# Float32 products of a retention and SiLU kernel as three one-pass products of 12-bit halves, in two parts

## The chip, the cores and the metric

The kernel runs on one core of one Trainium2 chip. The metric is the device time of one execution in microseconds (us); lower is better. The engines of a core run side by side, each through its own list of instructions in order: PE (TensorE, matmuls, with its weight loads shown apart as PEld), DVE (VectorE), ACT (ScalarE), POOL (GpSimd) and SP (SyncE, which here only issues DMAs). They wait for one another through semaphores.

## The reference

Attention by a recurrent state with decay, then a two-layer network with SiLU; B, H, S, D = 4, 8, 768, 64, d_model = 512, d_ff = 2048.

```python
for t in range(S):
    state = gamma * state + einsum('bhd,bhe->bhde', k[:, :, t], v[:, :, t])
    y[:, :, t] = scale * einsum('bhd,bhde->bhe', q[:, :, t], state)
x = y.transpose(0, 2, 1, 3).reshape(B * S, H * D)      # 3072 x 512
h = x @ w_in                                            # 512 x 2048
g = h * (1.0 / (1.0 + np.exp(-h)))
out = g @ w_out                                         # 2048 x 512
```

q, k, v are float32. The two weights arrive as float64 (a product of float32 noise with a float64 factor), so the kernel gets them as 64-bit words and rounds them to float32 itself.

## The kernel before

The 768 positions are cut into six chunks c of 128; a chunk of all four batches b is 512 tokens. A unit is one (c, b); its attention has four stages: `stage_t` (scaling of q on DVE and of v on POOL, transposes of k and q on PE, copies on ACT), `stage_a` (the scores, masked on DVE), `stage_y` (the output, transposed, copied into `xt[c]` by ACT) and `stage_s` (the update of the state on DVE; left out for the last chunk).

The network works in slices f of 128 of the 2048 hidden columns, 16 per chunk. `product_in(c, f)` makes h for a slice: four float32 matmuls of 128x128 weights with 128x512 tokens into one PSUM bank, then a sigmoid on ACT and one DVE multiplication give g. `product_out` multiplies a slice of g with the same slice of w_out, four matmuls into four banks `op[b]` that gather over all 16 slices; `store` copies them out at the end of a chunk. So per slice PE does eight float32 matmuls of 512 columns. In the trace each of them stands as two MATMUL records with two weight loads.

`product_out` runs one slice behind `product_in`, and one attention stage of chunk c + 1 stands after each slice of chunk c, so that a unit takes four slices. All weights stay on chip as float32 in `w_sb`, 16 tiles. `convert_w(f)` makes slice f of both weights out of the 64-bit words, eight DVE instructions over 1024 elements each; slices 0 to 3 are made during the attention of chunk 0 and the others during the 16 slices of chunk 0, four slices ahead of their use. Three staging tiles hold the words on their way in.

The order on each engine is set by the framework's scheduler from the order in which the code is written; on an engine nothing overtakes. Nearly all DMAs are issued by SP, in its order, and the stores of the result by ACT.

## Time and profile before

| | |
|---|---|
| time, 3 runs | 818.97 us median (816.91 to 819.06) |
| span of the profiled execution | 818.2 us |
| PE busy | 789.4 us, 96% of the span |
| DVE / ACT / POOL busy | 269.9 / 107.2 / 30.3 us |
| matmuls of the network, L263 and L273 | 768 + 768 records |
| DMA | 42.42 MB, mean 52 GB/s |

The span goes from the first to the last instruction, and the median of the runs is 0.8 us above it. A busy PE is not PE at its peak, since records of matmuls overlap; so the pace of a stream of matmuls is read from the chain of waits, where a group has the time that it advances the chain, and not from the mean of one record.

### The profile page before, as it was taken

How to read it: one execution, taken by the hardware profiler on the slowest of the kernel's cores; microseconds unless marked ns; L12 is line 12 of the kernel's file. 1: busy time of each engine (PE TensorE's matmuls, PEld its weight loads, DVE VectorE, ACT ScalarE, POOL GpSimd, SP SyncE). 2: the span in 40 equal slices, each digit the busy share in tenths (PEclk: the TensorE clock that was granted, in tenths of full speed). 3: DMA queues.
4: the chain of work that ended last, by engine and by line, in shares of the span. 5: the costliest groups of instructions: out<-in, count | busy, mean ns of one | idle time of the engine just before them, and what ended most of it. 6: DMA issues, size and time to landing. Idle time of an engine off the chain costs nothing.

```text
span 818.2 us, 7374 instructions
## 1 busy us (share of the span) xinstructions
PE 789.4 (96%) x3136; PEld 392.2 (48%) x3136; DVE 269.9 (33%) x398; ACT 107.2 (13%) x184; POOL 30.3 (4%) x36
## 2 busy tenths in 40 slices
PE   4789999999999999999999999999999999999997
PEld 3654445444544454545444544544454445444443
DVE  5889999922112112211122122111311111111111
ACT  1120111101111111011111110110111111100001
POOL 2100000000000000000000000000000000000000
PEclk9999999999999999999999999999999999999999
DMA  9868544102101103011011111000100000100001
GB/s 227 223 160 215 152 132 153 50 8 84 29 11 39 26 14 91 14 25 40 0 39 49 41 39 26 1 14 1 64 1 1 0 1 1 51 0 1 0 0 52
DMA packets 89121, 42.42 MB, mean 52 GB/s; under 512 B 75776, under 2 KB 83968, under 8 KB 89088
## 3 DMA queue, kind: packets, MB, share of 16 engines
q1 hardware_dynamic: 85632, 35.66, 17.5%
q10 hardware_dynamic: 3456, 6.29, 2.1%
q8 instruction: 24, 0.39, 0.2%
q14 instruction: 9, 0.07, 0.0%
HBM read 35.65 MB, written 6.29 MB: 51 GB/s over the span
## 4 chain that ended last, share of the span: by engine, by line
PE 84%; DVE 12%; issue 1%; DMA 1%; ACT 1%; SPq 0%; DVEq 0%; ACTq 0%
PE h L263 37%; PE op L273 35%; PE sc L205 3%; PE y L229 3%; PE y L225 2%; DVE w L137 2%; DVE ct L129 2%; DVE cp L133 2%; DVE ct L135 2%; PE s L243 1%; PE qtp L194 1%; PE ktp L194 1%; DVE ca L124 1%; DVE ca L122 1%; DVE am L211 1%
## 5 line engine op out<-in xcount | busy, mean ns | idle before, releaser
L263 PE MATMUL h<-xt,w 128*128 128x512 f32 x768 | 351.9, 601 | 0.0
L273 PE MATMUL op<-w,g 128*128 128x512 f32 x768 | 345.1, 593 | 0.0
L273 PEld LDWEIGHTS op<-w,g 128*128 128x128 f32 x768 | 146.2, 190 | 183.3 <-issue 182.2
L263 PEld LDWEIGHTS h<-xt,w 128*128 128x128 f32 x768 | 140.2, 191 | 154.0 <-issue 150.3
L268 DVE TENSOR_TENSOR g<-h,sg 128x512 f32<-128x512 f32 x96 | 66.3, 691 | 395.5 <-ACT sg L266 395.4
L266 ACT ACTIVATE sg<-h 128x512 f32<-128x512 f32 x96 | 57.3, 597 | 498.0 <-PE h L263 490.9
L229 PE MATMUL y<-am,vs 128*64 128x128 f32 x384 | 42.1, 299 | 10.3 <-DVE am L211 10.3
L188 POOL TENSOR_TENSOR vs<-vf,gk 128x512 f32<-128x512 f32 x24 | 27.5, 1144 | 599.4 <-PE s L243 530.2
L211 DVE TENSOR_TENSOR am<-sc,mask 128x512 f32<-128x512 f32 x48 | 31.3, 686 | 52.7 <-PE sc L205 52.7
L205 PEld LDWEIGHTS sc<-qt,kt 64*128 64x128 f32 x384 | 26.6, 210 | 19.6 <-issue 15.2
L229 PEld LDWEIGHTS y<-am,vs 128*64 128x64 f32 x384 | 28.7, 151 | 12.9 <-issue 9.2
L205 PE MATMUL sc<-qt,kt 64*128 64x128 f32 x384 | 31.6, 310 | 2.8 <-ACT qt L196 2.8
L225 PE MATMUL y<-qt,state 128*64 128x128 f32 x320 | 32.6, 279 | 0.0
L232 ACT COPY xt<-y 128x512 f32<-128x512 f32 x24 | 14.1, 586 | 124.5 <-PE y L229 124.5
L185 DVE TENSOR_TENSOR qs<-qf,gq 128x512 f32<-128x512 f32 x24 | 16.6, 690 | 38.1 <-PE qtp L194 37.5
L225 PEld LDWEIGHTS y<-qt,state 128*64 128x64 f32 x320 | 19.9, 136 | 15.2 <-issue 13.6
L250 DVE TENSOR_TENSOR state<-state,s 64x256 f32<-64x256 f32 x32 | 13.4, 417 | 36.1 <-PE s L243 35.6
L196 ACT COPY kt<-ktp 128x512 f32<-128x512 f32 x24 | 14.0, 585 | 66.7 <-PE ktp L194 66.7
L194 PE MATMUL ktp<-ident,kf 128*128 128x128 f32 x96 | 16.4, 299 | 5.4 <-DMA kf<-in_k_dram 5.4
L194 PE MATMUL qtp<-ident,qs 128*128 128x128 f32 x96 | 16.5, 300 | 5.1 <-DVE state L250 2.9
L194 PEld LDWEIGHTS ktp<-ident,kf 128*128 128x128 f32 x96 | 12.9, 154 | 16.3 <-issue 15.9
L243 PEld LDWEIGHTS s<-vs,kf 128*64 128x64 f32 x320 | 14.8, 154 | 12.1 <-issue 12.1
(32 smaller groups left out, 210.2 us busy)
## 6 DMA issues: line engine op xcount, KB each, us to landing
wf<-in_moe_w_in_dram SPq DMA_DIRECT2D x16, 512.0 KB, 4.3
wf<-in_moe_w_out_dram SPq DMA_DIRECT2D x16, 512.0 KB, 5.2
qf<-in_q_dram SPq DMA_DIRECT2D x24, 256.0 KB, 4.1
kf<-in_k_dram SPq DMA_DIRECT2D x24, 256.0 KB, 3.1
vf<-in_v_dram SPq DMA_DIRECT2D x24, 256.0 KB, 4.2
out_dram<-o ACTq DMA_DIRECT2D x24, 256.0 KB, 2.0
```

Source lines behind the costliest of these rows:

```text
L185: nc.vector.tensor_tensor(out=qs, in0=qf, in1=gq.unsqueeze(2).to_broadcast([128, H, D]), op=ALU.mult)
L188: nc.gpsimd.tensor_tensor(out=vs, in0=vf, in1=gk.unsqueeze(2).to_broadcast([128, H, D]), op=ALU.mult)
L194: nc.tensor.transpose(tp[:, a, :], src[:, 2 * a : 2 * a + 2, :], ident)
L205: nc.tensor.matmul(ap[j][:, a, :], lhsT=u["kt"][ts(j, D), a, :], rhs=u["qt"][ts(j, D), a, :], start=True, stop=True, skip_group_check=True)
L211: nc.vector.tensor_tensor(out=am, in0=ap[j], in1=mask.unsqueeze(1).to_broadcast([128, HP, C]), op=ALU.mult)
L225: nc.tensor.matmul(yp[ts(j, D), a, :], lhsT=state[b][:, a, ts(j, D)], rhs=u["qt"][:, a, :], start=True, stop=False, skip_group_check=True)
L229: nc.tensor.matmul(yp[ts(j, D), a, :], lhsT=u["vs"][:, 2 * a + j, :], rhs=u["am"][j][:, a, :], start=(c == 0), stop=True, skip_group_check ...
L243: nc.tensor.matmul(sp[ts(j, D), a, :], lhsT=u["kf"][:, h, :], rhs=u["vs"][:, h, :], start=True, stop=True, skip_group_check=True)
L263: nc.tensor.matmul(hp, lhsT=w_sb[f][:, 0, ts(kk, 128)], rhs=xt[c][:, kk, :], start=(kk == 0), stop=(kk == KIN - 1))
L266: nc.scalar.activation(out=sg, in_=hp, func=AF.Sigmoid)
L268: nc.vector.tensor_tensor(out=g, in0=hp, in1=sg, op=ALU.mult)
L273: nc.tensor.matmul(op[b], lhsT=g[:, ts(b, C)], rhs=w_sb[f][:, 1, :], start=(f == 0), stop=(f == NF - 1))
```

## The change

Every float32 value that goes into a product of the network is split into a high half of 12 bits and a low half, both held as `float32r`, a form of float32 that the tensor engine takes in one pass. With high h, low l and a scaled combination m, x @ w is built from three matmuls (h with h, l with the scaled low of w, and m with m), gathered in two PSUM banks, `ha` (`oa`) and `hb` (`ob`); the result is `ONE_E * ha - hb`. The attention keeps its float32 matmuls.

The kernel is cut in two. The first part makes g for all six chunks and writes it to DRAM (96 tiles of 128x512 float32); the second reads it back and makes the output. The 16 weight tiles `w{f}` (three 128x512 each) hold w_in's halves in the first part and w_out's in the second; w_out is rounded to float32 in the first part and also goes through DRAM.

```diff
+    def split_w(pool, f, w32, name):
+        w = wpool.tile([128, 3, 512], FP32R, tag=f"w{f}", name=f"{name}{f}")
+        lo = pool.tile([128, 512], FP32, tag="wl", name=f"{name}l_{f}")
+        nc.scalar.activation(out=w[:, 0, :], in_=w32, func=AF.Copy, scale=HALF)
+        high = w[:, 0, :].bitcast(FP32)
+        nc.vector.tensor_tensor(out=lo, in0=w32, in1=high, op=ALU.subtract)
+        nc.scalar.activation(out=w[:, 1, :], in_=lo, func=AF.Copy, scale=1.0 / EPS)
+        nc.vector.scalar_tensor_tensor(out=w[:, 2, :], in0=high, scalar=EPS, in1=lo,
+                                       op0=ALU.mult, op1=ALU.subtract)
...
-    ld = ctx.enter_context(tc.tile_pool(name="ld", bufs=4))
-    work = ctx.enter_context(tc.tile_pool(name="work", bufs=2))
-    stage = ctx.enter_context(tc.tile_pool(name="stage", bufs=3))
+        ld = first.enter_context(tc.tile_pool(name="ld", bufs=2))
+        one = first.enter_context(tc.tile_pool(name="one", bufs=1))
+        work = first.enter_context(tc.tile_pool(name="work", bufs=2))
+        stage = first.enter_context(tc.tile_pool(name="stage", bufs=2))
...
-    ps_a = ctx.enter_context(tc.tile_pool(name="ps_a", bufs=2, space=PS))
+        ps_a = first.enter_context(tc.tile_pool(name="ps_a", bufs=4, space=PS))
...
+        def take_w(i):
+            w32 = convert_w(i)
+            if i < NF:
+                w_sb[i] = split_w(conv, i, w32, "wi")
+            else:
+                nc.sync.dma_start(out=wo_dram[i - NF], in_=w32)
...
-        nc.scalar.copy(out=xt[c][:, :, ts(b, C)], in_=yp)
+            nc.scalar.activation(out=xh, in_=yp, func=AF.Copy, scale=HALF)
+            nc.vector.tensor_tensor(out=xl, in0=yp, in1=xh.bitcast(FP32), op=ALU.subtract)
+            nc.vector.scalar_tensor_tensor(out=xm, in0=xl.bitcast(FP32), scalar=-1.0 / EPS,
+                                           in1=xh.bitcast(FP32), op0=ALU.mult, op1=ALU.add)
...
-            nc.tensor.matmul(hp, lhsT=w_sb[f][:, 0, ts(kk, 128)], rhs=xt[c][:, kk, :],
-                             start=(kk == 0), stop=(kk == KIN - 1))
-        nc.scalar.activation(out=sg, in_=hp, func=AF.Sigmoid)
-        nc.vector.tensor_tensor(out=g, in0=hp, in1=sg, op=ALU.mult)
+                nc.tensor.matmul(ha, lhsT=w[0], rhs=x[0], start=first_, stop=False)
+                nc.tensor.matmul(ha, lhsT=w[1], rhs=x[1], start=False, stop=last)
+                nc.tensor.matmul(hb, lhsT=w[2], rhs=x[2], start=first_, stop=last)
+            nc.scalar.activation(out=hs, in_=ha, func=AF.Copy, scale=ONE_E)
+            nc.vector.tensor_tensor(out=hs, in0=hs, in1=hb, op=ALU.subtract)
+            nc.scalar.activation(out=g, in_=hs, func=AF.Sigmoid)
+            nc.gpsimd.tensor_tensor(out=g, in0=hs, in1=g, op=ALU.mult)
+            pending.append((c, f, g))
+        def put_g(keep):
+            while len(pending) > keep:
+                c, f, g = pending.pop(0)
+                nc.sync.dma_start(out=g_dram[c, f], in_=g)
...
-            if before is not None:
-                product_out(*before)
-                if f == 0:
-                    store(c - 1, before[0])
-            if c == 0:
-                convert_w(f + 4)
+                if c == 0 or f % 4 == 1:
+                    take_w(taken)
+                    taken += 1
+                put_g(1)
...
+        def split(n):
+            get(n + G_AHEAD)
+            if c == 0:
+                wo[f] = split_w(wl, f, got.pop((n, "w")), "wo")
+            nc.scalar.activation(out=t[:, 0, :], in_=g, func=AF.Copy, scale=HALF)
+            nc.vector.tensor_tensor(out=t[:, 1, :], in0=g, in1=high, op=ALU.subtract)
+            nc.vector.scalar_tensor_tensor(out=t[:, 2, :], in0=t[:, 1, :].bitcast(FP32),
+                                           scalar=-1.0 / EPS, in1=high,
+                                           op0=ALU.mult, op1=ALU.add)
...
+            for f in range(NF):
+                split(n + S_AHEAD)
+                for b in range(B):
+                    nc.tensor.matmul(oa[b], lhsT=gh, rhs=wo[f][:, 0, :], start=first_, stop=False)
+                    nc.tensor.matmul(oa[b], lhsT=glo, rhs=wo[f][:, 1, :], start=False, stop=last)
+                    nc.tensor.matmul(ob[b], lhsT=gm, rhs=wo[f][:, 2, :], start=first_, stop=last)
+            for b in range(B):
+                nc.scalar.activation(out=o, in_=oa[b], func=AF.Copy, scale=ONE_E)
+                nc.vector.tensor_tensor(out=o, in0=o, in1=ob[b], op=ALU.subtract)
+                nc.scalar.dma_start(out=out[ds(b * S + c * C, C), :], in_=o)
```

`convert_w` now takes half a slice at a time (512 elements; w_in first, then w_out): five instructions on one tensor (L158, L160, L163, L165, L169 of the kernel after) and three on two (L167, L171, L173). `get` reads a tile of g, and in chunk 0 one of w_out, three steps ahead; `split` runs two steps ahead of the matmuls.

PE before, at a slice of chunk 3 in which the scores of a unit stand (h: `product_in`, op: `product_out`, sc: scores):

```order
L263 MATMUL h_9_2401<-xt_1697,w_91 128x512 x4
L273 MATMUL op_3_2105<-w_90,g_8_2371 128x512
L273 MATMUL op_3_2106<-w_90,g_8_2371 128x512
L273 MATMUL op_3_2107<-w_90,g_8_2371 128x512
L273 MATMUL op_3_2108<-w_90,g_8_2371 128x512
L205 MATMUL sc_18_2414<-qt_2399,kt_2392 128x128
```

and now, at the same place:

```order
L239 MATMUL ktp_3235<-ident,kf_2886 128x128 x4
L239 MATMUL qtp_3242<-ident,qs_3231 128x128 x4
L318 MATMUL ha_9_3249<-xt_2298,wi_915 128x512
L319 MATMUL ha_9_3249<-xt_2298,wi_915 128x512
L320 MATMUL hb_9_3250<-xt_2298,wi_915 128x512
L318 MATMUL ha_9_3249<-xt_2298,wi_915 128x512
L319 MATMUL ha_9_3249<-xt_2298,wi_915 128x512
L320 MATMUL hb_9_3250<-xt_2298,wi_915 128x512
```

The eight matmuls of `product_in` and `product_out` became twelve of `product_in` alone (the rest of them read alike), and between the transposes of a unit and its scores, and between the scores and the output, stands one product, where two stood.

DVE before, in chunk 0 (ca, ct, cp: tiles of `convert_w`; w: its result; g: the SiLU):

```order
L131 TENSOR_SCALAR cp_615<-ct_614 128x1024
L268 TENSOR_TENSOR g_4_644<-h_4_637,sg_4_642 128x512
L133 SCALAR_TENSOR_TENSOR cp_615<-wf_472,cp_615 128x1024
L122 TENSOR_SCALAR ca_653<-wf_523 128x1024
L135 TENSOR_TENSOR ct_614<-ct_614,cp_615 128x1024
L124 TENSOR_SCALAR ca_653<-ca_653 128x1024
L137 SCALAR_TENSOR_TENSOR w_89<-wf_472,ct_614 128x1024
L268 TENSOR_TENSOR g_5_695<-h_5_688,sg_5_693 128x512
L127 TENSOR_SCALAR ct_654<-ca_653 128x1024
```

and now, also in chunk 0 (ca, cs, cp, cw: `convert_w`; wil, wi: `split_w`; hs: L323):

```order
L86 TENSOR_TENSOR wil_916<-cw_906,wi_915 128x512
L165 TENSOR_SCALAR ca_958<-ca_958 128x512
L88 SCALAR_TENSOR_TENSOR wi_915<-wi_915,wil_916 128x512
L167 SCALAR_TENSOR_TENSOR cs_959<-wf_836,ca_958 128x512
L323 TENSOR_TENSOR hs_7_1011<-hs_7_1011,hb_7_998 128x512
L169 TENSOR_SCALAR cp_960<-cs_959 128x512
L158 TENSOR_SCALAR ca_1019<-wf_901 128x512
L171 SCALAR_TENSOR_TENSOR cp_960<-wf_836,cp_960 128x512
L160 TENSOR_SCALAR ca_1019<-ca_1019 128x512
L173 TENSOR_TENSOR cw_961<-cs_959,cp_960 128x512
```

Instructions over 1024 elements became ones over 512, with the two of `split_w` between them. Of w_in all 16 halves are converted by slice 12 of chunk 0, and of w_out the last one in chunk 2.

SP before, at the end of its list (loads of q, k and v for the last units), and now, where the second part begins (gd: a store of g; wr: a load of w_out's slices, the first of which every matmul of the second part waits for):

```order
L79 DMA kf_2258<-in_k_dram 128x8x64
L79 DMA vf_2502<-in_v_dram 128x8x64
L79 DMA qf_2635<-in_q_dram 128x8x64
L79 DMA kf_2379<-in_k_dram 128x8x64
L79 DMA vf_2639<-in_v_dram 128x8x64
```

```order
L332 DMA gd_13_153<-g_13_4387 128x512 [waits DMAHW4_49,Pool_49]
L332 DMA gd_14_154<-g_14_4408 128x512 [waits DMAHW5_49,Pool_49]
L332 DMA gd_15_155<-g_15_4429 128x512 [waits DMAHW6_49,Pool_49]
L370 DMA wr_4460<-wod_156 128x512 [waits DMAHW7_49,Activation_49]
L370 DMA wr_4464<-wod_157 128x512 [waits DMAHW0_49]
```

The loads of w_out stand behind the store of the last tile of g, which waits for POOL; the first tiles of g for the second part are loaded in chunks 4 and 5 already, ahead of these.

## Rows read from the trace of the kernel before

**Rows 1.** The page: busy us (share) x instructions of each engine; GB/s in 40 slices

```profile
PE 789.4 (96%) x3136; PEld 392.2 (48%) x3136; DVE 269.9 (33%) x398; ACT 107.2 (13%) x184; POOL 30.3 (4%) x36
...
GB/s 227 223 160 215 152 132 153 50 8 84 29 11 39 26 14 91 14 25 40 0 39 49 41 39 26 1 14 1 64 1 1 0 1 1 51 0 1 0 0 52
```

**Rows 2.** Busy time in two stretches: us; PE, PEld, DVE, ACT, POOL (instructions); clock, DMA

```profile
0.00:160.00 160.00, 136.39 (x655) 76.88 (x656) 145.26 (x199) 23.81 (x40) 14.66 (x21) 1.00 0.64 166
182.00:312.00 130.00, 130.00 (x547) 63.87 (x543) 27.40 (x46) 17.27 (x30) 4.17 (x4) 1.00 0.13 33
```

**Rows 3.** The chain that ended last, 50 to 200 us: start us, us, what

```profile
60.62 1.22 DVE ct L129
...
155.22 1.14 DVE w L137
157.58 3.44 PE h L263 x8
```

**Rows 4.** The same chain, 196 to 232 us

```profile
198.08 3.63 PE h L263 x8
201.71 3.43 PE op L273 x8
...
214.11 0.62 PE s L243 x16
...
221.79 0.44 PE ktp L194 x4
...
229.53 1.09 PE sc L205 x16
230.62 1.49 PE h L263 x3
```

**Rows 5.** Weight loads one after another: start us, us, what [idle before <-releaser]

```profile
795.73 0.19 PEld L263 LDWEIGHTS h<-xt,w 128*128 128x128 f32 x1 [0.24 <-issue]
796.16 0.19 PEld L263 LDWEIGHTS h<-xt,w 128*128 128x128 f32 x1 [0.24 <-issue]
```

**Rows 6.** Groups on DVE by form: busy us, mean ns of one | idle before, releaser

```profile
L135 DVE TENSOR_TENSOR ct<-ct,cp 128x1024 f32<-128x1024 f32 x16 | 19.5, 1216 | 0.1
L122 DVE TENSOR_SCALAR ca<-wf 128x1024 uint32<-128x1024 uint32 x16 | 11.8, 738 | 6.0 <-DMA wf<-in_moe_w_out_dram 6.0
L127 DVE TENSOR_SCALAR ct<-ca 128x1024 uint32<-128x1024 uint32 x16 | 11.0, 686 | 0.1
L268 DVE TENSOR_TENSOR g<-h,sg 128x512 f32<-128x512 f32 x96 | 66.3, 691 | 395.5 <-ACT sg L266 395.4
L250 DVE TENSOR_TENSOR state<-state,s 64x256 f32<-64x256 f32 x32 | 13.4, 417 | 36.1 <-PE s L243 35.6
L252 DVE TENSOR_TENSOR state<-state,gc 64x256 f32<-64x256 f32 x32 | 14.7, 459 | 0.9
```

**Rows 7.** The start on DVE: start us, us, what [idle before <-releaser]

```profile
10.98 0.69 DVE L122 TENSOR_SCALAR ca<-wf 128x1024 uint32<-128x1024 uint32 x1 [6.04 <-DMA wf<-in_moe_w_out_dram]
```

**Rows 8.** The staged weights: us from issue to landing

```profile
DMA to landing us min/median/max: 3.8/5.0/7.0
```

**Rows 9.** Groups on ACT and POOL, as rows 6

```profile
L266 ACT ACTIVATE sg<-h 128x512 f32<-128x512 f32 x96 | 57.3, 597 | 498.0 <-PE h L263 490.9 <-DVE ct L135 7.1
L188 POOL TENSOR_TENSOR vs<-vf,gk 128x512 f32<-128x512 f32 x24 | 27.5, 1144 | 599.4 <-PE s L243 530.2 <-issue 30.7 <-PE y L229 23.8
```

**Rows 10.** DMA issues of the result: number, KB each, median us to landing

```profile
out_dram<-o ACTq DMA_DIRECT2D x24, 256.0 KB, 2.0
```

**Rows 11.** The scores of one unit on PE, at the start and later: start us, us

```profile
8.05 2.08 PE L205 MATMUL sc<-qt,kt 64*128 64x128 f32 x16 [0.67 <-ACT qt L196]
...
424.69 1.16 PE L205 MATMUL sc<-qt,kt 64*128 64x128 f32 x16
```

**Rows 12.** The last matmuls: start us, us

```profile
810.75 2.31 PE L273 MATMUL op<-w,g 128*128 128x512 f32 x5
```

More of the change, by code (lines that the diff above doesn't have):

```diff
@@ L66 @@
-    ps_h = ctx.enter_context(tc.tile_pool(name="ps_h", bufs=2, space=PS))
-    ps_o = ctx.enter_context(tc.tile_pool(name="ps_o", bufs=1, space=PS))
-    units = [(c, b) for c in range(NC) for b in range(B)]
-    loaded = {}
-    def load(n):
-        if n >= len(units):
-            return
-        c, b = units[n]
-        tiles = []
-        for name, src in (("q", q), ("k", k), ("v", v)):
-            t = ld.tile([128, H, D], FP32, tag=f"{name}f", name=f"{name}f_{n}")
-            nc.sync.dma_start(out=t, in_=src[b, :, ds(c * C, C)].rearrange("h t d -> t h d"))
-            tiles.append(t)
-        loaded[n] = tiles
@@ L140 @@
[L140 to L143 removed]
+    def split_w(pool, f, w32, name):
[7 more added lines that the diff above has]
+                                       op0=ALU.mult, op1=ALU.subtract)
+        return w
@@ L208, in stage_a @@
[L208 to L226 removed]
+                nc.vector.memset(gc[ts(j, D), a, :], math.exp(C * lg[2 * a + j]))
@@ new lines, in stage_a @@
+        def stage_a(n):
+            u = live[n]
+            ap = [bank(f"sc{j}_{n}").rearrange("p (a t) -> p a t", a=HP) for j in range(2)]
+            for a in range(HP):
+                for j in range(2):
+                    nc.tensor.matmul(ap[j][:, a, :], lhsT=u["kt"][ts(j, D), a, :],
+                                     rhs=u["qt"][ts(j, D), a, :], start=True, stop=True,
+                                     skip_group_check=True)
+            u["am"] = []
+            for j in range(2):
+                am = one.tile([128, HP, C], FP32, tag=f"am{j}", name=f"am{j}_{n}")
+                nc.vector.tensor_tensor(out=am, in0=ap[j],
+                                        in1=mask.unsqueeze(1).to_broadcast([128, HP, C]),
+                                        op=ALU.mult)
+                u["am"].append(am)
@@ L227, in stage_y, with stage_s @@
+        def stage_s(n):
+            c, b = units[n]
+            u = live.pop(n)
+            if c == NC - 1:
+                return
+            sp = bank(f"s_{n}")[:, : HP * D].rearrange("p (a e) -> p a e", a=HP)
+            for a in range(HP):
+                for j in range(2):
+                    h = 2 * a + j
+                    nc.tensor.matmul(sp[ts(j, D), a, :], lhsT=u["kf"][:, h, :],
+                                     rhs=u["vs"][:, h, :], start=True, stop=True,
                                      skip_group_check=True)
@@ L271, in product_out @@
-    def product_out(op, f, g):
-        for b in range(B):
-            nc.tensor.matmul(op[b], lhsT=g[:, ts(b, C)], rhs=w_sb[f][:, 1, :],
-                             start=(f == 0), stop=(f == NF - 1))
-    def store(c, op):
-        for b in range(B):
-            o = work.tile([128, DM], FP32, tag="o", name=f"o_{c}_{b}")
-            if b % 2:
-                nc.vector.tensor_copy(out=o, in_=op[b])
-            else:
-                nc.scalar.copy(out=o, in_=op[b])
-            nc.scalar.dma_start(out=out[ds(b * S + c * C, C), :], in_=o)
@@ L304, with attend @@
-    product_out(*before)
-    store(NC - 1, before[0])
+                st = state[b][ts(j, D), :, ts(j, D)]
+                src = sp[ts(j, D)]
+                if c > 0:
+                    nc.vector.tensor_tensor(out=st, in0=st, in1=src, op=ALU.add)
+                    src = st
+                nc.vector.tensor_tensor(out=st, in0=src,
+                                        in1=gc[ts(j, D)].to_broadcast([D, HP, D]), op=ALU.mult)
+        stages = (stage_t, stage_a, stage_y, stage_s)
+        def attend(c, step):
+            stages[step % 4](c * B + step // 4)
```

365 lines of the change are left out of this document (200 added, 165 removed).

## The prediction

> **What bounds the kernel now.** I read the engines' busy times first, then the chain that ended last, then two stretches of it, then the groups of each engine. PE is busy for 96% of the span and DVE for 33% [rows 1], but that is a mean over two stages. In the first 160 us DVE is busy for 145.3 us [rows 2], and from 60 to 157 us the chain runs through the conversion of the weights on DVE, from one piece of `convert_w` to the next [rows 3]: that stage is DVE's. From 157.6 us on the chain is PE alone, and there DVE is busy for 27.4 of 130 us [rows 2]: that stage is PE's. So the change has to be costed stage by stage: fewer passes help only where PE sets the pace, and each new DVE instruction counts in chunk 0.
>
> **What a product costs now.** Eight records of `product_out`, four float32 products, advance the chain by 3.43 us [rows 4]: 0.429 us a record and 0.857 us a product. [...] The reader is to see that nothing of the weight loads is in this: a load takes 0.19 us, the next starts 0.43 us after it [rows 5], which is the record's own pace. Four slices, 198.08 to 230.62 us, take 32.54 us; eight groups of products take 8 x 3.43 = 27.44, which leaves 5.10 us for the attention of a unit with all its handovers [rows 4].
>
> [...] A slice of either product becomes 12 matmuls of one pass. No row shows a one-pass matmul of 512 columns. The bounds: half a record, 0.2144 us, if loads stay hidden, and a whole record, 0.429 us, if the new form saves nothing. I take 0.2144: a load of 0.19 us still fits under it, and four transposes, each a load of 128 columns and a matmul of 128, advance the chain by 0.44 us, 0.11 us each [rows 4], so that loads can follow one another at twice the pace that is needed. A slice is then 12 x 0.2144 = 2.573 us and 16 slices 41.2 us; before, 54.9 us.
>
> [...]
>
> **Chunk 0, on DVE.** An operation on two tensors takes 1.216 us for 1024 elements and 0.691 for 512 [rows 6], so 0.166 plus 1.03 ns an element. One on a single tensor takes 0.686 to 0.738 for 1024 [rows 6]: about half the price an element, so 0.43 for 512 (0.426 to 0.452). From the order, up to the last L323 of chunk 0, DVE has 93 of these, 40.0 us; 142 of two tensors at 0.69, 98.0 us (54 of the conversion, 32 of `split_w`, 16 of L323, 16 of L279 and L280, 16 masks, 8 scalings of q); 20 updates of the state at 0.417 or 0.459 [rows 6], 8.9 us; and 2.6 us of constants: 149.5 us. That is hardly less than now, because the halves of w_out no longer all come here (18 half slices for 32) and `split_w`, L323, L279 and L280 take that back. Before, DVE lost 160 - 145.3 = 14.7 us in this stage, 6.0 of them waiting for the first weights [rows 2, 7]; these now stand behind 0.79 MB of q, k and v alone and not behind the first slice of w_in too, 0.52 MB less, 2.3 us at the 227 GB/s of the start [rows 1], so 12.4 lost. I add 6 us for SP: there are two staging tiles for three, a load lands after 3.8 to 7.0 us [rows 8], DVE comes back to a tile after about 7 us, and some of these loads stand on SP behind a load of k that waits for PE. Both ends: 0, and 2 us for each of 18, 36. Chunk 0 ends at 149.5 + 12.4 + 6 = 168 us. PE is not the bound there: 16 x (2.573 + 5.10 / 4) = 62 us of work.
>
> **Chunks 1 to 5 of the first part.** PE needs 41.2 + 4 x 5.10 = 61.6 us a chunk. In chunk 1 DVE has 46 x 0.43 + 64 x 0.69 + 7.0 = 71 us, nine half slices of w_out among it, and is the bound; both are loaded, so plus 5: 76. In chunk 2 DVE has 21 x 0.43 + 51 x 0.69 + 7.0 = 51 us, PE is the bound: 61.6 + 3. Chunk 3: 61.6. Chunk 4 has no `stage_s`, 4 x 0.62 less [rows 4]: 59.1. Chunk 5 has no attention: 41.2 + 1. ACT has two instructions of 0.597 a slice and three a unit, POOL one of 1.144 a slice and one a unit [rows 9], 6.6 and 5.7 us of the 15.4 of a unit: hidden, and if POOL took twice that, still hidden. The first part ends on PE at 168 + 76 + 64.6 + 61.6 + 59.1 + 42.2 = 471.5 us.
>
> **Between the parts.** After the last product come ACT 0.6, DVE 0.69, ACT 0.6, POOL 1.14 [rows 6, 9], then on SP the store of the last g and behind it the first load of w_out, which lands after 2.0 (as the stores of 256 KB [rows 10]) to 3.8 us [rows 8], then ACT 0.6 and two of DVE at 0.69: 7.0 to 8.8 us with no matmul, plus five handovers. At the start the scores of a unit took 2.08 us and later 1.16 [rows 11], about half the pace, though the clock column says 1.00 in both; should PE start slow again, the first 2 to 4 us of work cost double. I take 10 us; the ends are 7 and 14.
>
> **The second part.** 96 slices x 2.573 = 247.0 us. DVE has two instructions a slice, 1.38 us, and in chunk 0 four, 2.76, over PE's 2.57; but the first three tiles of g are split before the part begins, so it keeps ahead. Its 25 MB of g come at 0.26 MB per 2.57 us, 100 GB/s; the first 160 us now move 166 GB/s [rows 2], so they are hidden. At the end of a chunk the four pairs of banks are emptied one after another while PE works on the later ones: 0.3 us each, 1.5 in all (upper end 2 us each, 10). The end: now 818.2 - 813.1 = 5.1 us [rows 12] for a copy and a store; 5 again.
>
> **Sum.** 471.5 + 10 + 247.0 + 1.5 + 5 = 735.0 us of span, against 818.2. With the 0.8 us by which the median stands over the span: 736. The gain is in chunks 2 to 5 and in the second part, none of it in chunk 0.
>
> **Rivals.** (a) *DVE and SP hold the first part longer.* For it: DVE is 90% busy in chunk 0 by the sum, and between scores and output now stands one product of 2.57 us, for two of 7.06. Against: the masks are ready 0.6 + 0.69 + 2 x 0.69 + 0.2 = 2.9 us after the product ahead of them, and the output is due after 1.09 + 2.57 = 3.7. Price: the other 30 of the 36 in chunk 0 and 1.5 us for each of 16 units, 24: 790, and half of it 763. (b) *Weight loads show.* [...] If load and matmul followed one another, a transpose's 0.11 would be a load of 0.057 and a matmul of 0.053; the pair is then 0.271, and with all of 0.11 beyond the pass 0.324. Counted in chunks 2 to 5 and the second part, 160 slices of 12: 1920 x 0.057 = 109 to 1920 x 0.11 = 211, with chunk 1 turning to PE's, so 845 to 950 us. It is slower than now from 0.044 us a matmul on, (819 - 736) / 1920. Against: rows 5. (c) *The new form is no faster than a record*, 0.429: 160 slices x 2.57 more and 50 in chunks 0 and 1, some 1190 us. (d) *Hardly any stall*: no idle DVE in chunk 0 but for the first weights, none at the seams: 736 - 12 - 8 - 10, some 706.
>
> **How the numbers follow.** Forecast 0.66 (710 to 763), (a) 0.16 (763 to 790), (b) 0.09, (c) 0.04, (d) 0.05. The range 710 to 790 leaves out (b), (c) and (d), 0.18 in all. A measurement of this kernel can tell 0.3%, 2.5 us, from no change. Faster: 0.66 + 0.16 + 0.05 = 0.87; slower: (b) and (c) but for the 0.01 in which (b) lies at its turning point, 0.12; same 0.01.
>
> **What would show it.** L318 to L320 and L409 to L411 advance the chain by 0.214 us a matmul: (b) and (c) are out. Chunk 0 ends near 168 us with the chain on DVE, chunk 1 near 244, the first part near 471; a gap of 8 to 10 us without matmuls follows; in the second part the chain is PE at 41 us a chunk. I am wrong if matmuls come at 0.24 us or more with PE waiting for nothing, if the conversion waits for its loads in most slices, or if PE waits for DVE in chunks 3 and 4.

## The result, and the profile of the changed kernel

The changed kernel takes **766.6 us** (764.6 to 767.0), against 818.9 us before: a ratio of 0.936, 95% interval 0.935 to 0.938. The forecast was 736 us. The profiled execution has a span of 765.3 us for 818.2.

The page of the changed kernel, the busy time of each engine and the chain that ended last (it answers [rows 1]):

```profile
PE 691.3 (90%) x3904; PEld 545.6 (71%) x3904; DVE 518.8 (68%) x842; ACT 268.8 (35%) x452; POOL 159.9 (21%) x132
...
PE 60%; issue 16%; DVE 13%; POOL 7%; DMA 2%; ACT 1%; SPq 0%; POOLq 0%; DVEq 0%; ACTq 0%
```

The share of "issue" is idle time ahead of POOL's g in the first part: the chain is followed back from the start of the second part through the last g's, one after another. PE is busy there all the time, as the next view shows, so it is not what bounds these chunks.

The same by stages (it answers [rows 2]). The first six stretches end with the last L323 of each chunk of the first part; the last two are the first chunk of the second part and its other five. Columns: the stretch, its length, busy us and instructions of PE, PEld, DVE, ACT and POOL, the granted clock, DMA share, GB/s:

```profile
0.00:164.40 164.40, 115.48 (x725) 83.48 (x726) 146.34 (x274) 55.38 (x93) 36.58 (x36) 0.88 0.52 138
164.40:244.40 80.00, 71.81 (x470) 54.10 (x469) 77.31 (x127) 24.11 (x42) 26.56 (x20) 0.91 0.60 188
244.40:316.70 72.30, 68.18 (x476) 53.49 (x475) 56.76 (x89) 25.44 (x45) 25.24 (x20) 0.95 0.46 140
316.70:381.90 65.20, 65.20 (x482) 51.53 (x481) 34.59 (x53) 25.85 (x45) 24.91 (x21) 1.00 0.38 114
381.90:444.90 63.00, 63.00 (x422) 50.47 (x421) 28.86 (x41) 26.50 (x45) 24.23 (x20) 1.00 0.33 104
444.90:489.60 44.70, 43.56 (x186) 34.67 (x185) 15.05 (x21) 20.52 (x34) 21.15 (x16) 1.00 0.31 114
495.90:542.30 46.40, 46.36 (x193) 37.90 (x194) 39.53 (x64) 28.72 (x50) 0.00 (x0) 0.94 0.52 154
542.30:759.90 217.60, 217.60 (x961) 179.97 (x959) 119.04 (x178) 59.87 (x97) 0.00 (x0) 1.00 0.37 115
```

DVE fills the first two chunks, as forecast. In chunks 0 to 2 PE waits in places, and its granted clock is 0.88, 0.91 and 0.95, where the stage on DVE had 1.00 before [rows 2]; the forecast has no term for that. From chunk 3 on PE waits for nothing, and yet every stretch is longer than forecast. The stretches set against the terms of the sum, in us:

| stretch | forecast | measured | difference |
|---|---|---|---|
| chunk 0 | 168 | 164.4 | -3.6 |
| chunk 1 | 76 | 80.0 | +4.0 |
| chunk 2 | 64.6 | 72.3 | +7.7 |
| chunk 3 | 61.6 | 65.2 | +3.6 |
| chunk 4 | 59.1 | 63.0 | +3.9 |
| chunk 5 | 42.2 | 44.7 | +2.5 |
| between the parts | 10 | 6.3 | -3.7 |
| second part | 248.5 | 264.0 | +15.5 |
| the end | 5 | 5.4 | +0.4 |
| span | 735.0 | 765.3 | +30.3 |

The forecast ends the first part with its last product, the table with the last L323: counted as in the forecast, the first part ends at 488.3 us for 471.5, and 7.6 us lie between the parts for 10.

The largest term is the second part, where nothing but products is left. The timeline of PE, start and length of matmuls in us, in chunk 5 of the first part (470 us) and in the second part (600 us):

```profile
469.79 0.40 PE L320 MATMUL hb<-xt,wi 128*128 128x512 f32 x1
...
471.90 0.39 PE L320 MATMUL hb<-xt,wi 128*128 128x512 f32 x1
...
600.07 0.39 PE L409 MATMUL oa<-wo,gs 128*128 128x512 f32 x1
...
600.75 0.39 PE L409 MATMUL oa<-wo,gs 128*128 128x512 f32 x1
```

From 600.07 to 600.75 lie three products of the second part: **0.2267 us** each, and they keep this pace (217.6 us for five chunks of 192 in the last stretch above). The first two lines, nine products apart, give 2.11 / 9 = 0.2344 us in the first part, and over the 177 products of chunk 5 from 446 to 487 us it is **0.2343 us**. The forecast had 0.2144, half a record of [rows 4], for both. In the trace each of these matmuls is one record: 384 of L318 for 6 x 16 x 4.

How one part follows the other: the last product of the first part and the first of the second on PE's timeline, and the chain of waits between them: start us, us, what:

```profile
488.07 0.40 PE L320 MATMUL hb<-xt,wi 128*128 128x512 f32 x1
495.94 1.65 PE L409 MATMUL oa<-wo,gs 128*128 128x512 f32 x3 [7.47 <-ACT wo L84]
```

```profile
491.67 0.32 SPq L332
...
492.08 3.07 DMA wr<-wod
...
495.26 0.64 ACT wo L84
...
498.98 0.43 PE ob L411
...
501.85 0.23 PE oa L410
```

From the last product, which starts at 488.07 and ends 0.23 us later, to 495.94 no matmul runs, 7.6 us. The links are those that were forecast (POOL's last g, the store, the load of w_out, ACT), without the two instructions of DVE at the end: the first matmul waits for the high half of w_out alone, and that is ACT's. Then matmuls come 0.43 us apart until 501.5, with a granted clock of 0.50; after that the clock is 1.00 and the spacing 0.23. That makes the first chunk of the second part 46.4 us long instead of 43.5. Together 10.5 us, where the forecast had 10 for gap and slow start.

### The profile page after: what moved, and what is told of

It reads as the page before. It is cut to its first block, busy times and chain, and to the rows that moved or that the text cites. A ratio compares the mean times of both kernels' runs of the same rounds, so it can differ in the third digit from the quotient of the medians.

```text
span 765.3 us, 10695 instructions
## 1 busy us (share of the span) xinstructions
PE 691.3 (90%) x3904; PEld 545.6 (71%) x3904; DVE 518.8 (68%) x842; ACT 268.8 (35%) x452; POOL 159.9 (21%) x132
## 4 chain that ended last, share of the span: by engine, by line
PE 60%; issue 16%; DVE 13%; POOL 7%; DMA 2%; ACT 1%; SPq 0%; POOLq 0%; DVEq 0%; ACTq 0%
PE oa L409 11%; PE oa L410 11%; PE ob L411 11%; POOL g L326 6%; PE ha L318 6%; PE hb L320 5%; PE ha L319 5%; PE y L274 3%; PE sc L250 2%; PE y L270 2%; DVE hs L323 2%; DVE am L256 1%; DVE cs L167 1%; DVE state L301 1%; PE s L292 1%
## 5 line engine op out<-in xcount | busy, mean ns | idle before, releaser
L326 POOL TENSOR_TENSOR g<-hs,g 128x512 f32<-128x512 f32 x96 | 131.4, 1369 | 248.0 <-ACT g L325 243.3
L318 PE MATMUL ha<-xt,wi 128*128 128x512 f32 x384 | 164.0, 428 | 15.1 <-ACT wi L84 13.5
L319 PE MATMUL ha<-xt,wi 128*128 128x512 f32 x384 | 158.2, 412 | 7.4 <-ACT wi L87 5.7
L320 PE MATMUL hb<-xt,wi 128*128 128x512 f32 x384 | 153.2, 414 | 4.3 <-DVE hs L323 3.5
L409 PE MATMUL oa<-wo,gs 128*128 128x512 f32 x384 | 150.2, 392 | 7.5 <-ACT wo L84 7.5
L410 PE MATMUL oa<-wo,gs 128*128 128x512 f32 x384 | 150.4, 392 | 0.0
L411 PE MATMUL ob<-wo,gs 128*128 128x512 f32 x384 | 150.3, 391 | 0.0
L323 DVE TENSOR_TENSOR hs<-hs,hb 128x512 f32<-128x512 f32 x96 | 65.7, 685 | 93.5 <-ACT hs L322 93.2
L318 PEld LDWEIGHTS ha<-xt,wi 128*128 128x128 f32 x384 | 74.6, 195 | 39.2 <-ACT wi L84 16.5
L319 PEld LDWEIGHTS ha<-xt,wi 128*128 128x128 f32 x384 | 75.6, 197 | 25.9 <-ACT wi L87 8.2
L320 PEld LDWEIGHTS hb<-xt,wi 128*128 128x128 f32 x384 | 75.0, 198 | 26.1 <-DVE hs L323 5.7
L409 PEld LDWEIGHTS oa<-wo,gs 128*128 128x128 f32 x384 | 72.6, 189 | 23.1 <-ACT wo L84 7.9
L410 PEld LDWEIGHTS oa<-wo,gs 128*128 128x128 f32 x384 | 72.7, 189 | 15.6 <-ACT wo L87 0.5
L411 PEld LDWEIGHTS ob<-wo,gs 128*128 128x128 f32 x384 | 72.6, 189 | 15.0
L388 DVE SCALAR_TENSOR_TENSOR gs<-gs 128x512 fp32r<-128x512 f32 x96 | 66.8, 700 | 2.4
```

Source lines behind the costliest of these rows:

```text
L318: nc.tensor.matmul(ha, lhsT=w[0], rhs=x[0], start=first_, stop=False)
L319: nc.tensor.matmul(ha, lhsT=w[1], rhs=x[1], start=False, stop=last)
L320: nc.tensor.matmul(hb, lhsT=w[2], rhs=x[2], start=first_, stop=last)
L323: nc.vector.tensor_tensor(out=hs, in0=hs, in1=hb, op=ALU.subtract)
L326: nc.gpsimd.tensor_tensor(out=g, in0=hs, in1=g, op=ALU.mult)
L388: nc.vector.scalar_tensor_tensor(out=t[:, 2, :], in0=t[:, 1, :].bitcast(FP32), scalar=-1.0 / EPS, in1=high, op0=ALU.mult, op1=ALU.add)
```

## Experiments on the pace of a product

Three readings of 0.2267 instead of 0.2144: the load of the weights shows, each matmul has a fixed cost, or switching between the two accumulators costs. The first run changes the second part, each chunk in another way; chunks 0 and 1 stay. Half of the output's rows (chunk 2), half of its columns (chunk 3), one accumulator (chunk 4) and the high half of g in all three products (chunk 5) are not what the layer asks for.

```diff
+            rows = C // 2 if c == 2 else C
+            cols = DM // 2 if c == 3 else DM
...
-                    gh, glo, gm = (t[:, i, ts(b, C)] for i in range(3))
+                    gh, glo, gm = (t[:, 0 if c == 5 else i, ds(b * C, rows)] for i in range(3))
+                    pa = oa[b][:rows, :cols]
+                    pb = pa if one_bank else ob[b][:rows, :cols]
```

> Second part only, one change per chunk: chunks 0 and 1 as they are (0.2267 us from matmul to matmul), chunk 2 with weights of 64 columns in place of 128 (half of the output rows left out), chunk 3 with 256 moving columns in place of 512 (half of the output columns left out), chunk 4 with all three matmuls into one bank, chunk 5 with the high half of g as weights of all three (other values). Theory A, the pass waits for the weight load under it: chunk 2 goes to 0.214 or less over its pass (0.213), chunk 3 hardly falls and stays at 0.19 to 0.227. Theory B, a fixed 13 ns is added to each matmul: chunk 2 stays at 0.227, chunk 3 falls to 0.107 + 0.013 = 0.120 within a slice. Theory C, the change of PSUM banks costs it: chunk 4 alone falls to 0.214. Under A and B chunks 4 and 5 stay at 0.227.

It took 746.5 us. PE's timeline in it, with 64 columns of weights (600 us) and with 256 moving columns (640 us):

```profile
599.73 0.39 PE L417 MATMUL oa<-wo,gs 128*64 128x512 f32 x1
...
601.11 0.39 PE L417 MATMUL oa<-wo,gs 128*64 128x512 f32 x1
...
639.75 0.28 PE L417 MATMUL oa<-wo,gs 128*128 128x256 f32 x1
...
640.95 0.28 PE L419 MATMUL ob<-wo,gs 128*128 128x256 f32 x1
```

Six matmuls with the smaller load take 1.38 us, 0.230 each: 3 ns more and not less, although the load itself fell from 0.188 to 0.134 us. Ten of 256 columns take 1.20 us, 0.120 each. The chunk with one accumulator took 43.6 us, 0.227 a product. So neither load nor accumulator sets the pace. From 256 to 512 columns a matmul gains 0.1067 us, 0.417 ns a column, so 0.2133 us for 512; what stays at both widths is **0.0133 us for each matmul**. What makes it was not found. The chunk with one weight tile for all three products kept 0.2267 as well.

The first part is slower by another 0.0076 us. The next run leaves out work around its last chunk, four slices at a time: first the store of g, then POOL's g too, then DVE's part of hs as well.

```diff
-            nc.vector.tensor_tensor(out=hs, in0=hs, in1=hb, op=ALU.subtract)
+            if c < NC - 1 or f < 12:
+                nc.vector.tensor_tensor(out=hs, in0=hs, in1=hb, op=ALU.subtract)
...
+            if c < NC - 1 or f < 8:
+                nc.gpsimd.tensor_tensor(out=g, in0=hs, in1=g, op=ALU.mult)
+            if c < NC - 1 or f < 4:
+                pending.append((c, f, g))
```

> Chunk 5 of the first part, where matmuls come every 0.234 us, in four steps: slices 0 to 3 as they are, 4 to 7 without the store of g, 8 to 11 also without the multiplication on POOL, 12 to 15 also without the subtraction on DVE (so chunk 5 of the output is not computed; the second part reads the g of chunk 4 there). Theory A, traffic of other engines or DMAs in SBUF makes the 0.234 out of the 0.227 of the second part: the pace falls to 0.227 at one of the steps, and that step names the cause. Theory B, it lies in the matmuls themselves (their operands' places): 0.234 in all sixteen slices. The rest of the kernel as in the kernel after, 760 to 767 us.

It took 764.6 us. The engines in its third group of slices, and two products there:

```profile
467.00:478.00 11.00, 11.00 (x49) 8.84 (x48) 2.69 (x4) 4.77 (x8) 1.29 (x1) 1.00 0.00 0
```

```profile
471.67 0.39 PE L320 MATMUL hb<-xt,wi 128*128 128x512 f32 x1
...
472.84 0.40 PE L319 MATMUL ha<-xt,wi 128*128 128x512 f32 x1
```

With no DMA and one instruction of POOL and four of DVE in 11 us, five products still take 1.17 us, 0.234 each, as in the other three groups. So the extra is in the product. The next run varies its operands, two slices of chunk 5 at a time:

```diff
+                w = [w_sb[f][:, 0 if v in (2, 7) else i, ts(0 if v in (4, 7) else kk, 128)]
+                     for i in range(3)]
+                x = [xt[c][:, 0 if v in (1, 7) else i, 0 if v in (3, 7) else kk, :]
+                     for i in range(3)]
+                if v == 6:
+                    x = [w_sb[i][:, i, :] for i in range(3)]
```

> Only the products of the last chunk of the first part differ, two slices for each variant, so what it computes there is not the layer's: slices 0-1 as they are; 2-3 the same moving tile for all three products; 4-5 the same weight tile for all three; 6-7 the moving tile of kk 0 for every kk; 8-9 the weights of kk 0 for every kk; 10-11 each product in two of 256 columns; 12-13 the moving operand read from w_in's tiles; 14-15 one pair of operands for all. In the first part a product takes 0.2343 us, in the second 0.2267. Theory 'where the operands lie' (the extra 7.6 ns belongs to addresses of moving or weight operand): at least one of 2-3, 4-5, 6-7, 8-9, 12-13 or 14-15 falls to about 0.227. Rival 'something outside the product' (the queue that feeds TensorE, other engines' traffic): all but 10-11 stay at 0.234. For 10-11: a fixed cost of some 13 to 21 ns for each product, so 0.120 to 0.128 us each. Total within 3 us of the changed kernel, 763 to 768 us.

764.1 us. In slices 0 to 9 and 14, 15 every product took 0.234 us. One variant fell, slices 12 and 13, whose moving operand is read from w_in's tiles; and 256 columns out of xt cost 0.117 each, half of 0.234, so that the 0.0133 us do not show there:

```profile
469.77 0.28 PE L328 MATMUL ha<-xt,wi 128*128 128x256 f32 x1
...
470.59 0.28 PE L329 MATMUL hb<-xt,wi 128*128 128x256 f32 x1
...
475.72 0.39 PE L329 MATMUL hb<-wi,wi 128*128 128x512 f32 x1
...
476.85 0.39 PE L328 MATMUL ha<-wi,wi 128*128 128x512 f32 x1
```

Seven in 0.82 us; five in 1.13 us, 0.226. So it hangs on the moving operand, and xt differs from w_in's tiles in at least three things: where it starts within 64 bytes, how far into SBUF it lies, and what it holds. Two runs shift tiles by 32 bytes:

```diff
+        pad = const.tile([128, 8], FP32, tag="pad", name="pad")
+        nc.vector.memset(pad, 0.0)
```

> One tile of 32 bytes a partition is added ahead of the constants' others, so that every later tile of the first part, xt (the moving operand of its products) among them, lies 32 bytes further on: xt begins on a multiple of 64 bytes, where it began 32 bytes past one. Nothing else. Theory 'the address of the moving operand': a product of the first part takes 0.2267 us, as in the second, instead of 0.2343: 1.46 us for each chunk of 192 products where the products set the pace, so chunk 5 of the first part 43.3 us instead of 44.7, chunks 3 and 4 shorter by 1 to 1.5, and 759 to 764 us. Rival 'what xt holds, or how it was written': 0.234 us as before, 764 to 768 us.

763.9 us (762.1 to 767.7), not to be told from the changed kernel's 766.6; a product of the first part fell by 0.001, to 0.2333 us. The theory of the 64 bytes asked for 0.2267 and falls. The other run has the same tile in the pool of w_in and w_out:

> The same 32 bytes, ahead of w_in's and w_out's tiles instead: these tiles and the second part's g, its high and low parts (gs) now begin 32 bytes past a multiple of 64, while xt begins on one. Nothing else. Theory 'the address of the moving operand': the second part's products, whose moving operand is now the shifted one (w_out), take 0.234 us instead of 0.2267, 8.8 us in all, and its chunks 45.0 us instead of 43.5; the first part's, whose weights alone are now shifted, 0.2267: 768 to 773 us. Rival 'the address of the weights' (or of either operand): 0.234 us in the first part as well, 772 to 778 us. Rival 'what the operands hold': 0.234 and 0.227 as before, 764 to 768 us.

768.4 us (764.9 to 774.9), with 0.2342 us in the first part and 0.2267 in the second, as without a shift: w_out, now the one off the 64 bytes, is read no slower, and xt, on a multiple of 64 here too, no faster. The time lies where the first theory had it, but its pace does not. The last run copies one of w_in's tiles to where xt's neighbours lie, and a piece of xt to where w_in's tiles lie, and lets chunk 5 read these:

```diff
+                    nc.scalar.activation(out=w_high[0], in_=w_sb[3][:, 0, :].bitcast(FP32),
+                                         func=AF.Copy)
...
+                    nc.scalar.activation(out=w_sb[0][:, 0, :],
+                                         in_=xt[c][:, 0, 0, :].bitcast(FP32), func=AF.Copy)
+                other = (None, w_high[0], w_sb[0][:, 0, :], w_sb[1][:, 0, :])[f // 4]
```

> Only the moving operand of the last chunk's products in the first part differs, four slices for each variant, so what it computes there is not the layer's: slices 0-3 as they are (xt); 4-7 a copy of one of w_in's tiles, in the stage's buffer, 202 kB into a partition; 8-11 a copy of a piece of xt, in w_in's first tile, 17 kB in; 12-15 a tile of w_in where it lies, 23 kB in. xt lies from 149 kB on. The runs so far leave two readings of the 7.6 ns by which a product is longer in the first part. Theory 'the place' (the moving operand is read slower from high addresses of SBUF): 0.234, 0.234, 0.227, 0.227 us for the four. Rival 'what the operand holds' (xt's values, not its place): 0.234, 0.227, 0.234, 0.227. Total 763 to 768 us either way, since the whole chunk differs by under 1.5 us.

764.5 us. PE's timeline in it, first w_in's values read from 202 kB into a partition, then xt's values from 17 kB:

```profile
459.79 0.40 PE L334 MATMUL hb<-whigh,wi 128*128 128x512 f32 x1
...
460.96 0.39 PE L333 MATMUL ha<-whigh,wi 128*128 128x512 f32 x1
...
469.74 0.39 PE L332 MATMUL ha<-wi,wi 128*128 128x512 f32 x1
...
471.10 0.39 PE L332 MATMUL ha<-wi,wi 128*128 128x512 f32 x1
```

Five in 1.17 us, 0.234; six in 1.36, 0.2267. **The pace went with the place of the moving operand, not with its values**: w_in's took 0.234 us at 202 kB, xt's 0.2267 at 17 kB. Of the 0.0076 us at most 0.001 is the 64 bytes. The weights lay in w_in's tiles, low, in every variant. No place between 115 kB (the end of w_in's tiles) and 149 kB (xt) was tried. Nor is the extra a second fixed cost on top of the first: 256 columns take 0.117 us from xt and 0.120 from w_out's tiles. How the two combine stays open.

Float32 does not show the place. In chunk 1 of the kernel before xt begins at 149 kB, and the moving operand of `product_out`, w_out, lies below 82 kB; eight records of either product advance the chain alike:

```profile
222.66 3.44 PE h L263 x8
226.10 3.43 PE op L273 x8
```

## Experiments on DVE and POOL in the first chunks

Chunks 1 and 2 came out 12 us over their terms, while the pace explains 3.8. What DVE and POOL did in chunk 1 of the changed kernel, from their timelines:

```profile
191.28 1.35 POOL L326 TENSOR_TENSOR g<-hs,g 128x512 f32<-128x512 f32 x1 [4.29 <-ACT g L325]
194.25 1.27 POOL L326 TENSOR_TENSOR g<-hs,g 128x512 f32<-128x512 f32 x1 [1.62 <-ACT g L325]
```

```profile
190.45 0.42 DVE L160 TENSOR_SCALAR ca<-ca 128x512 f32<-128x512 f32 x1
190.78 0.69 DVE L230 TENSOR_TENSOR qs<-qf,gq 128x512 f32<-128x512 f32 x1
191.39 1.52 DVE L163 TENSOR_SCALAR ca<-ca 128x512 uint32<-128x512 uint32 x1
...
194.36 1.70 DVE L167 SCALAR_TENSOR_TENSOR cs<-wf,ca 128x512 uint32<-128x512 uint32 x1
```

The instruction of DVE that starts inside POOL's g ends 0.3 to 0.5 us after it: 1.52 us instead of 0.42, and 1.70 instead of 0.69. Why they take longer, the trace does not show. The test: the same product on DVE, which costs DVE 16 more instructions a chunk and frees it of POOL.

```diff
-            nc.gpsimd.tensor_tensor(out=g, in0=hs, in1=g, op=ALU.mult)
+            nc.vector.tensor_tensor(out=g, in0=hs, in1=g, op=ALU.mult)
```

> The multiplication that makes g goes from POOL back to DVE, 0.69 us more of DVE in each slice. Theory A, POOL's work lengthens DVE's instructions (in the kernel after, an update of the state takes 0.79 us for the 0.46 of before, L167 0.85 for 0.69): these go back to 0.46 and 0.70, DVE loses about as much as it gains in chunks 0 and 1, and the time is 758 to 770 us. Theory B, they are lengthened by something else: they stay at 0.79 and 0.85, chunks 0 and 1 grow by 16 x 0.69 = 11 us each and chunk 2 by some 6, and the time is 785 to 797 us.

**743.3 us** (741.5 to 744.2), a ratio of 0.908 to the kernel before, interval 0.906 to 0.910: 23 us faster than the changed kernel, well below what was expected: the direction was right, the size too small. Groups of DVE by form in the first 245 us, in this kernel and then in the changed one, busy us and mean ns of one:

```profile
L163 DVE TENSOR_SCALAR ca<-ca 128x512 uint32<-128x512 uint32 x27 | 11.6, 430 | 0.1
L323 DVE TENSOR_TENSOR hs<-hs,hb 128x512 f32<-128x512 f32 x35 | 23.9, 683 | 0.6 <-ACT hs L322 0.4
```

```profile
L323 DVE TENSOR_TENSOR hs<-hs,hb 128x512 f32<-128x512 f32 x32 | 21.7, 679 | 0.6 <-ACT hs L322 0.3
...
L163 DVE TENSOR_SCALAR ca<-ca 128x512 uint32<-128x512 uint32 x28 | 18.1, 645 | 0.1
```

L163 goes from 645 to 430 ns, as do its like (L158, L160, L165 and L169 to some 420), while L323, one of whose operands comes from PSUM, was no longer beside POOL's g (679 ns) than without it (683). Chunks 0, 1 and 2 end at 161.6, 230.1 and 295.3 us: 80.0 became 68.5, and 72.3 became 65.2. With POOL free, DVE does more and ends earlier. Of the 7.1 us of chunk 2, some 3 had been the lower clock (68.18 us of PE busy, at 0.95, for 65.20 in chunk 3) and 4 PE's waits; in this run its clock is 1.00 there.

The other edit takes work from DVE in chunks 0 and 1: w_out's pieces go to chunks 1 to 4, one in four slices.

```diff
-                if c == 0 or f % 4 == 1:
+                if (c == 0 and taken < NF) or (1 <= c < NC - 1 and f % 4 == 1):
```

> The 16 halves of w_out are converted evenly, one per four slices of chunks 1 to 4 (their result in a tile of the ring of g, so that they cannot be drawn forward), in place of 2 in chunk 0, 9 in chunk 1 and 5 in chunk 2. Theory A, DVE is what holds chunks 0 and 1 and part of chunk 2: chunk 0 ends about 9 us earlier, chunk 1 falls from 80 to 66 us, chunk 2 from 72 to 67, chunks 3 and 4 grow by 1 or so; the time is 736 to 745 us. Theory B, PE waits there for other things (loads on SP, handovers): chunks 1 and 2 stay above 72 and 70, and the time is 758 to 768 us.

**736.9 us** (736.1 to 739.1), ratio 0.901, interval 0.900 to 0.903. Its chunks 0 and 1:

```profile
0.00:158.20 158.20, 114.59 (x713) 82.38 (x714) 137.54 (x261) 54.08 (x91) 36.71 (x36) 0.85 0.52 138
158.20:223.30 65.10, 64.49 (x475) 50.58 (x474) 56.97 (x91) 25.62 (x44) 24.93 (x20) 1.00 0.52 162
```

Chunk 1 is now 65.1 us long and PE is busy for 64.5 of it; chunks 2 and 3 take 65.2 each. That is PE's own time for a chunk with attention at the full clock, 1.00 here. What chunks 1 and 2 had over it was PE's waits for DVE, with the lower clock in these chunks, 0.91 and 0.95.

## Experiments on the seam, on the cut alone, and all together

The conversion of w_out's tiles is moved from the first chunk of the second part into the last of the first, into the same buffers:

```diff
+                if c == NC - 1:
+                    if f >= 2:
+                        wo[f - 2] = split_w(conv, f - 2, wo32.pop(f - 2), "wo")
+                    get_wo(f)
```

> The conversion of w_out into its three tiles is moved from the first chunk of the second part into the last chunk of the first part, into the same SBUF. Nothing is left out. Theory 'the seam' (the 7.65 us without a matmul between the parts is the load and the two-engine conversion of the first w_out tile and the loads of the first g; the half clock that follows costs another 2.9 us; and the first chunk of the second part is longer than the others, 46.4 against 43.5 us, for the same reasons): the gap falls to about 4 us (one trip of the last g through DRAM stays), 755 to 761 us. Rival 'POOL and DVE have no room in chunk 5': the 16 conversions (DVE two instructions of about 0.69 and 0.79 us each) delay the hs and g of the last slices, chunk 5 of the first part grows from 44.7 us to above 50, and the time stays at 763 to 770.

**758.6 us** (758.2 to 760.6), ratio 0.928, interval 0.927 to 0.930. The seam in its chain of waits:

```profile
489.01 0.61 ACT hs L331
...
489.64 0.70 DVE hs L332
...
490.38 0.50 PE oa L416
490.88 0.23 PE oa L417
```

The last product of the first part starts at 488.75, so the gap is 1.4 us, not the 4 expected: the second part begins with g of chunk 0, which lies in DRAM long since, and the trip of the last g holds up nobody; what held the start was w_out. What is left is the wait for the last hs. After this pause the granted clock stays at 1.00, the first chunk takes 43.7 us, and chunk 5 grew by 0.9.

What the change does without the halves: the changed kernel with single float32 products. It keeps the cut in two, and g's product on POOL.

```diff
-                nc.tensor.matmul(ha, lhsT=w[0], rhs=x[0], start=first_, stop=False)
-                nc.tensor.matmul(ha, lhsT=w[1], rhs=x[1], start=False, stop=last)
-                nc.tensor.matmul(hb, lhsT=w[2], rhs=x[2], start=first_, stop=last)
+                nc.tensor.matmul(ha, lhsT=w_sb[f][:, ts(kk, 128)], rhs=xt[c][:, kk, :],
+                                 start=kk == 0, stop=kk == KIN - 1)
```

> The structure of the changed kernel (two parts, g through DRAM, the same order of slices and stages), but with single float32 products in place of the three one-pass ones, and no halves. Nothing is left out. It tells what the cut alone does. Theory 'the cut is paid for by itself and buys nothing': the time of the kernel before plus the gap between the parts, less what the w_out products no longer share with the stages: 815 to 835 us, with 0.429 us a record in both parts, no gain. Rival 'the cut itself brings part of the gain' (short accumulators, less waiting): under 805 us.

**838.7 us** (835.9 to 841.8), ratio 1.026, interval 1.023 to 1.028: a little over the range given. Its chunks 0, 1 and 3 and its second part:

```profile
0.00:132.70 132.70, 102.18 (x641) 61.61 (x641) 117.85 (x223) 43.04 (x75) 32.38 (x35) 0.94 0.68 177
132.70:223.40 90.70, 80.58 (x417) 43.17 (x418) 75.07 (x127) 25.32 (x45) 27.42 (x20) 0.94 0.61 185
...
298.60:373.90 75.30, 75.30 (x417) 39.69 (x418) 18.72 (x29) 25.31 (x46) 25.05 (x21) 1.00 0.34 99
...
501.00:834.00 333.00, 329.49 (x768) 145.54 (x766) 8.29 (x12) 8.65 (x15) 1.27 (x1) 1.00 0.31 92
```

This structure alone **costs 21 us**. PE has the same work as before (789.9 us for 789.4), but half of it can no longer lie beside the conversion in chunk 0, where PE now waits 30.5 us, and another 10 in chunk 1. Not all of that need be the cut: g is on POOL here too, and the instruction that is L163 in the changed kernel takes 543 ns on average in these two chunks, for the 430 that it takes without POOL's g. A run of the cut with g on DVE was not made. From this kernel to the changed one the time falls by 72 us: the second part's products from 329.5 us to 264.0, chunk 3 from 75.3 to 65.2; chunk 0 loses 31.7 to the splits on DVE (132.7 to 164.4).

Then the three edits that each gained, at once:

> Three edits at once: the sixteen w_out pieces that the first chunk read and turned are taken in chunks 1 to 4, g's product on DVE instead of POOL, and w_out's conversion in chunk 5 of the first part. Nothing is left out. If the three costs are separate places (chunk 0 to 2 bounded by DVE instructions that are longer beside POOL and by the w_out work; the seam): 736.9 of the late w_out alone, less about 9 for the seam and about 3 for a shorter chunk 0: 722 to 729 us. If chunk 5 cannot take the conversions beside g on DVE, or the edits take away the same microseconds: 731 to 737 us.

**725.7 us** (724.0 to 726.6), ratio 0.887, interval 0.885 to 0.888. One by one they gave 23, 30 and 8 us; together 41 and not 61, since the first two free the same two chunks of DVE, which then end on PE. With the 32 bytes ahead of the constants as well:

> The three edits of the last run at 725.7 us (w_out's pieces taken in chunks 1 to 4, g's product on DVE, w_out's conversion in the last chunk of the first part), with the 32 bytes that put xt on a multiple of 64. Nothing is left out. If the products set the pace from chunk 1 on, as the chunks of 65 us in that run say, and the address sets the products: five chunks of 192 products by 7.6 ns, 7.3 us, and a part of chunk 0's: 717 to 720 us. If the address is not the cause: 724 to 727 us.

**720.3 us** (720.0 to 724.2), ratio 0.882, interval 0.879 to 0.884: the best of all that was run, 46 us under the changed kernel. The time is near the one expected, but its reason was wrong. Chunk 0 of this kernel, and of the one without the shift:

```profile
0.00:147.90 147.90, 102.68 (x705) 74.10 (x706) 132.02 (x274) 54.72 (x91) 13.31 (x21) 0.93 0.53 144
```

```profile
0.00:154.30 154.30, 111.05 (x705) 81.33 (x706) 132.62 (x273) 54.51 (x91) 12.19 (x21) 0.86 0.52 138
```

The later chunks are shorter by at most 0.3 us each (chunk 1: 65.4 for 65.6), and a product of the first part takes 0.2333 us, not 0.2267. The gain is 6.4 us in chunk 0, with the same work on DVE, 0.93 of the clock for 0.86, and 8.4 us less of PE busy. The clock differs from one execution to the next of the same kernel, and the time goes with it: the execution of this kernel with 0.971 over the whole span took 724.2 us and one of the kernel without the shift with 0.971 took 724.0, while the two executions with 0.985 took 720. So nothing here shows a gain of the shift at the same clock; whether the shift makes the higher clock more frequent is open.

## Why the prediction was right in its direction and 30 us short

**The mechanism held.** A product went from 0.857 us to three matmuls of 0.2267 us in the second part and 0.2343 in the first, and a smaller load made them no shorter (0.230); the gain is in the later chunks and the second part, none in chunk 0; the gap between the parts and the slow start behind it cost 10.5 us for the 10 forecast. Rivals (b) and (c) are out by the pace, (d) by the seams and by chunks 1 and 2.

**The term that was too small: the pace of a product**, "I take 0.2144". It was bounded from below by half a record, and that bound was taken. That the new form takes half a float32 record was the author's estimate: no run shows 0.2144 us for a matmul of 512 columns, the runs showed 0.2267 and 0.2343. In the second part 1152 x 0.0123 = 14.2 us (and 2.9 for the lower clock at its start, which the forecast had put into the gap); in chunks 3 to 5 3 x 192 x 0.0199 = 11.5, and 3.8 in chunk 2: 29.5 us, for 30.3 measured. The other terms miss by up to 4 us each, in both directions, and cancel; that the rest comes out at under 1 us is luck. The extra was looked for in the loads (rival b), where it is not (0.230 us with half of the weight columns): it is 0.0133 us for each matmul in the second part, and in the first the pace goes with where xt lies, 0.2343 us and 0.2267 lower down. The records of before could not show it: they take 0.429 us from either place, and so they do in both parts of the kernel without the halves. The fixed cost and the place were measured on the new form alone. The turning point, 0.044 us a matmul, was far off.

**The step that failed: "hidden, and if POOL took twice that, still hidden".** POOL was hidden, as an engine that someone waits for, but no engine was costed as held up by it. Beside its g DVE's instructions are longer (L163 645 ns, without it 430), and chunks 1 and 2 together came out 11.7 us over their terms; 3.8 of that is the pace. The rest, some 8, goes with POOL's g or with DVE's load, for either edit brings chunk 2 to 65.2, and in chunk 2 some 3 of it are the lower clock.

**A term that was right by luck.** For chunk 0 the sum of DVE's instructions was 149.5 us; 146.3 were busy, by two errors that cancel. Lengths in the trace overlap: an instruction of 0.69 us is followed by the next after 0.61, one of 0.42 after 0.33 (190.78 and 190.45 above). The 274 lengths of chunk 0 add up to 163.4 us, 17 more than were busy; the trace of before has the same, 156.9 us of lengths in the first 160 us for 145.3 busy [rows 2]. And POOL lengthens them by some 15: with g on DVE the lengths other than those of g add up to 148.6, which is what the forecast had. The idle time, forecast at 12.4 + 6 = 18.4, was 164.4 - 146.3 = 18.1, and that is luck too: the 6 us for later loads of w_in's words did not occur (DVE waited for such a load once, for the first, 6.0 us), while some 6 us of waits for ACT and 3 for PE did.

**The rest.** Chunk 5 had 1 us beyond its products in the forecast and has next to nothing. The seams inside the second part, forecast at 1.5 us, don't show: 217.6 us are 960 products at 0.2267.

**Against the rivals' prices.** 766.6 us lies outside the forecast's own 710 to 763 and within (a)'s 763 to 790. But (a) named staging tiles and the attention's waits for it, priced up to 54 us; of its kind are the some 8 us in chunks 1 and 2, and chunk 0, its main place, came out early. So the measured time lies in (a)'s range by luck, not by (a)'s cause. None of the three signs of being wrong showed: matmuls came at 0.2343 us and not at 0.24, which is close, the conversion waited for one load, and PE did not wait for DVE in chunks 3 and 4.

## What to carry to other kernels

A duration in the trace is not a price: take the spacing from one start to the next, for DVE (0.61 us for 0.69) as for PE (0.2267 for 0.39), and do not take half a record of one form for the pace of another (0.2144 us forecast, 0.2267 and 0.2343 measured). Before a product goes to POOL because POOL is idle, look at what DVE does at that time: here moving it back to the busier engine made the kernel 23 us faster. Where a loop is cut in two, find the work of the second loop that lay beside the first one's bottleneck; here the structure with the cut cost 21 us, part of it perhaps g on POOL, and preparing the second part inside the first gave 8 back. And where PE waits for another engine, look at its granted clock in that stretch: in chunk 2 a clock of 0.95 cost some 3 us of its own.
